# Reading K and V in runs of 32 KB that each fill two SBUF partitions

## The chip, the cores and the metric

The kernel runs on one core of one Trainium2 chip. The metric is the device time of one execution in microseconds (us); each of three runs is one time, and the median stands for the kernel. The profile is a separate execution of the same program; it counts from the first to the last instruction (its "span").

## The reference

A decode step of two branches that a gate mixes: attention over the last 2,048 keys of a cache, and a small MLP. Only the attention part reads much: K and V of 8 batches and 16 KV heads, 2,048 x 128 bf16 values each, 134.2 MB together.

```python
B, Sq, D, F = 8, 1, 576, 4608
Hq, Hkv, Sk, Dh = 32, 16, 8192, 128
W = 2048                                   # min(4096, max(256, Sk // 4))
g = sigmoid((x * gate_w).sum(-1, keepdims=True))
q = (x @ wq).reshape(B, Sq, Hq, Dh).transpose(0, 2, 1, 3)
k = repeat(k_cache[:, :, Sk - W:, :], 2, axis=1)
v = repeat(v_cache[:, :, Sk - W:, :], 2, axis=1)
p = softmax(einsum("bhqd,bhkd->bhqk", q, k) * Dh ** -0.5)
a = einsum("bhqk,bhkd->bhqd", p, v).transpose(0, 2, 1, 3).reshape(B, Sq, Hq * Dh) @ wo
b = gelu(layernorm(x) @ w1 + b1) @ w2 + b2
out = g * a + (1 - g) * b
```

## The kernel before

All SBUF data lie in one tensor, the arena. Its largest part, RAW, is cut into nine slots (`NSLOT`) of 16 KB in each of the 128 partitions, 2 MiB a slot. Everything large is streamed through these slots by loads that SyncE (SP) issues, in the order of the list `stream` (L549 to L560): five K units, then K and V units by turns, a quarter of wo (1,152 KB) behind every eighth V unit, and at the end b2 and four pieces of w2. wq and w1 are loaded first and lie where the first slots will be. SP issues a load as soon as its slot is free (`slot_free`), so several loads wait in the DMA engines' queues at any time.

One unit is one load of 2 MiB: four batches (`a`) of one KV head, 2,048 keys of 128 bf16 values each. There are 32 K units and 32 V units. `src_of` (L575) describes the source: for one batch and head the 2,048 keys are contiguous in HBM (512 KB), and it cuts them into 32 blocks `x` of 64 keys (16 KB), block outermost, batch next. The destination is a whole slot, 128 rows of 16 KB. Element order pairs the two: partition 4x + a holds block x of batch a. Both sides of one piece are 16 KB: one contiguous run in HBM, one row of the slot. A load's semaphore is complete when it has risen by 16.

A K unit (`k_unit`, L624) is transposed on VectorE in 32 x 32 blocks, half a slot at a time (L642, two instructions), and multiplied on TensorE with a block-diagonal q into PSUM (L656 to L659; the held matmuls carry the helper's line, L173). Since a row of 32 partitions holds several batches, the four heads and batches that don't belong together are pushed to a large negative score before the first K unit of a group of four: a matmul of `maskL` and `maskR` (L651). `maskR` is built once on GpSimd (L364) by an affine select over 512 columns whose pattern says to which batch a column belongs: 128 times the batches 0 to 3, one column each. Softmax follows per group of four K units (L584 to L622). A V unit (`v_unit`, L671) is used untransposed: 16 matmuls (L682) of the transposed probabilities with the slot. K and V lie in the same partition order, so the probabilities and V's rows agree.

The order on each engine comes from a planner (`_Plan.schedule`), which uses costs and due times; the loads keep the order of `stream` by `after=last_dma`.

Of the kernel before, what the change touches and what calls it, by code (L numbers as in the profile page):

```python
# [9 lines left out]
ALU = mybir.AluOpType  # L10
# [28 lines left out]
class _Plan:  # L39
# [10 lines left out]
    def add(self, eng, fn, deps=(), name=None, cost=0.1, after=(), prio=0):  # L50
        op = _Op(eng, fn, deps, name, cost, after=after, prio=prio)
        op.idx = len(self.all)
        self.all.append(op)
        return op
# [122 lines left out]
        tile_size=tile_size, tile_position=tile_position, ldweights=False))  # L177


def build_kernel(nc, A_x, A_k_cache, A_v_cache, A_wq, A_wo, B_x, B_w1, B_b1, B_w2, B_b2, gate_w, out):  # L180
    B, Sq, D = A_x.shape
    _, Hkv, Sk, Dh = A_k_cache.shape
    Hq = A_wq.shape[1] // Dh
    F = B_w1.shape[1]
    W = min(4096, max(256, Sk // 4))
    assert Sq == 1 and Dh == 128 and B == 8 and W == 2048 and Hq == 2 * Hkv and Hkv == 16
    assert D == 576 and F == 4608
    S0 = Sk - W
# [4 lines left out]
    SE = 4 * W  # L193
# [11 lines left out]
    with ExitStack() as es:  # L205
# [64 lines left out]
        AST = _pst(arena)  # L270
        arena_f = arena.bitcast(F32)

        def aoffs(name):
            return R[name][0] // 2
# [12 lines left out]
        ones_bf = view("ones_bf")  # L287
# [37 lines left out]
        def slot(s):  # L325
            return RAW[:, s * SE:(s + 1) * SE]

        wq_m = RAW[:, 0:4 * 4096].rearrange("p (t c) -> p t c", t=4)
        wq_r = RAW[:, 4 * 4096:4 * 4096 + 2048]
        W1O = 3 * SE  # L330
# [3 lines left out]
        def col(i, parts=128):  # L334
# [26 lines left out]
        o_xz0 = add("pool", lambda e: e.memset(view("xz", 8), 0.0), name="xz0", cost=0.2)  # L361
        o_yz0 = add("pool", lambda e: e.memset(view("yz", 8), 0.0), name="yz0", cost=0.2)
        o_z = add("pool", lambda e: e.memset(zeros_bf, 0.0), name="zeros", cost=0.15)
        o_mR = add("pool", lambda e: e.affine_select(out=maskR, in_=ones_bf, pattern=[[0, 128], [1, 4]], compare_op=ALU.is_equal,  # L364
                                                     fill=0.0, base=0, channel_multiplier=-1), deps=[o_ones], name="maskR", cost=0.8, prio=-1)
        o_mL = add("pool", lambda e: e.affine_select(out=maskL, in_=zeros_bf, pattern=[[0, 16], [1, 4], [0, 2]], compare_op=ALU.is_equal,
                                                     fill=-BIG, base=0, channel_multiplier=-1), deps=[o_z], name="maskL", cost=0.4, prio=-1)
# [206 lines left out]

        def src_of(cache, g, q):  # L575
            hkv, b0 = 2 * g + q // 2, 4 * (q % 2)
            return cache[b0:b0 + 4, hkv, S0:Sk, :].rearrange("a (x r) d -> x a (r d)", x=32)

        def take_slot():
            n = n_slot[0]  # L580
# [43 lines left out]
        def k_unit(i):  # L624
            g, q = divmod(i, 4)
            s = take_slot()
            d = dma("sp", lambda e: e.dma_start(slot(s), src_of(A_k_cache, g, q)), "s%d" % s, 4 * W * Dh * 2, deps=slot_free[s], name="dk%d" % i, after=last_dma[-1:])
            last_dma.append(d)
            ub = q
            qrs = []  # L630
            for a in range(4):
                def fn(e, a=a):
                    dst = bass.AP(arena, offset=32 * a * AST + aoffs("qbd") + ub * 512 + 32 * a + 8 * q, ap=[[AST, 32], [128, 4], [1, 8]])
                    src = bass.AP(arena, offset=32 * a * AST + aoffs("q4") + 32 * g + 8 * q, ap=[[AST, 32], [256, 4], [1, 8]])
                    return e.tensor_copy(dst, src)  # L635
                qrs.append(add("pool", fn, deps=[o_q4, o_qz] + [qk_unit.get(i - 4)], name="qr%d_%d" % (i, a), cost=0.2))
            trs = []
            for h in range(2):
                n = 2 * i + h
                kb = n % 2  # L640
                deps = [d] + ([qk_half[n - 2]] if n >= 2 else [o_y, o_ssq])
                tr = add("dve", (lambda h=h, kb=kb: lambda e: e.transpose(bass.AP(arena_f, offset=foffs("KT") + kb * 2048, ap=[[AST // 2, 128], [1, 2048]]),  # L642
                                                                         bass.AP(arena_f, offset=foffs("RAW") + s * (SE // 2) + 32 * h, ap=[[AST // 2, 128], [64, 64], [1, 32]])))(),
                         deps=deps, name="tr%d_%d" % (i, h), cost=2.3, after=tr_hist[-1:])
                tr_hist.append(tr)
                trs.append(tr)

                def qk_fn(e, h=h, kb=kb):
                    mm = None
                    if q == 0 and h == 0:  # L650
                        e.matmul(ps[:, 0, :], maskL, maskR, start=True, stop=False)  # L651
                        for rc in range(1, 4):
                            held_matmul(nc, e, ps[:, rc, :], maskL, maskR, start=True, stop=False)
                    for ee in range(2):
                        for rc in range(4):
                            rhs = bass.AP(arena, offset=aoffs("KT") + kb * 4096 + rc * 1024 + ee, ap=[[AST, 128], [2, 512]])  # L656
                            args = (ps[:, rc, :], qbd[:, ub, 2 * h + ee, :], rhs)
                            last = q == 3 and h == 1 and ee == 1
                            mm = e.matmul(*args, start=False, stop=last) if rc == 0 else held_matmul(nc, e, *args, stop=last)  # L659
                    return mm  # L660
                deps = [tr] + qrs
                if q == 0 and h == 0:
                    deps += exp_done[g - 1] if g else [o_q4, o_mL, o_mR]
                qk = add("pe", qk_fn, deps=deps, name="qk%d_%d" % (i, h), cost=1.95 + (0.9 if q == 0 and h == 0 else 0), after=qk_half[-1:])
                qk_half.append(qk)
            qk_unit[i] = qk
            slot_free[s] = trs
            if q == 3:
                softmax(g)

        def v_unit(i):  # L671
            g, q = divmod(i, 4)
            s = take_slot()
            item = 2 * g + q // 2
            d = dma("sp", lambda e: e.dma_start(slot(s), src_of(A_v_cache, g, q)), "s%d" % s, 4 * W * Dh * 2, deps=slot_free[s], name="dv%d" % i, after=last_dma[-1:])  # L675
            last_dma.append(d)

            def pv_fn(e):
                mm = None
                for t in range(16):  # L680
                    c = 32 * (t % 4)
                    mm = e.matmul(ps[c:c + 32, BK_OS[i % 2], :], PT[:, g % 2, 512 * q + 32 * t:512 * q + 32 * t + 32], slot(s)[:, 512 * t:512 * t + 512],  # L682
                                  start=(t < 4), stop=(t >= 12), skip_group_check=True, tile_position=(0, c))
                return mm
            deps = [d] + pt_done[g] + ([u_ev[i - 2]] if i >= 2 else [o_qT, o_u])
            prev = add("pe", pv_fn, deps=deps, name="pv%d" % i, cost=1.5, after=pv_hist[-1:])
            pv_hist.append(prev)
            slot_free[s] = [prev]
            if q == 3:
                pv_last[g] = prev  # L690
            u_ev[i] = add("act", lambda e: e.activation(out=EV[:, i % 2, :], in_=ps[:, BK_OS[i % 2], :], func=ACTF.Copy),  # L691
                          deps=[prev] + ([u_sum[i - 2]] if i >= 2 else []), name="uev%d" % i, cost=0.8, prio=3)

            def us_fn(e):
                mm = None
                for r in range(4):
                    mm = e.matmul(ps[:, BK_S, OC + 16 * (item % 2) + 8 * (q % 2):OC + 16 * (item % 2) + 8 * (q % 2) + 8], EV[:, i % 2, 128 * r:128 * r + 128], i32[:, 8 * r:8 * r + 8],  # L697
                                  start=(r == 0), stop=(r == 3), skip_group_check=True)
                return mm
            u_sum[i] = add("pe", us_fn, deps=[u_ev[i]] + o_i32 + b6_r[-2:], after=b6_w[-1:], name="us%d" % i, cost=1.0, prio=3)  # L700
            b6_w.append(u_sum[i])
            if q % 2 == 1:
                hl = q // 2
                prev = u_sum[i]
                osrc = ps[:, BK_S, OC + 16 * (item % 2):OC + 16 * (item % 2) + 16]
                if item < Hkv - 1:
                    ev = add("act", lambda e: e.activation(out=o32[:, item % 2, :], in_=osrc, func=ACTF.Copy), deps=[prev] + ([oT_done[item - 2]] if item >= 2 else []), name="oev%d" % item, cost=0.25, prio=3)  # L707
                    o_item_ev[item] = ev
                    b6_r.append(ev)
                    eng, src_, deps = "pool", o32[:, item % 2, :], [ev, rg_done[g]]  # L710
                else:
                    eng, src_, deps = "dve", osrc, [prev, rg_done[g]]

                def om_fn(e):
                    return e.tensor_tensor(out=oT[:, item, :, :].rearrange("p h b -> p b h"), in0=src_.rearrange("p (b h) -> p b h", h=2),  # L715
                                           in1=rg[:, g % 2, 16 * hl:16 * hl + 16].rearrange("p (b h) -> p b h", h=2), op=ALU.mult)
                oT_done[item] = add(eng, om_fn, deps=deps, name="oT%d" % item, cost=0.25, prio=9)
# [120 lines left out]
```

## Time and profile before

| | |
|---|---|
| median of 3 runs | 369.54 us (369.46 to 369.54) |
| profiled execution: span | 367.9 us; what lies around the span is not in the profile, and the page states no other time of this execution |
| bytes read from HBM | 154.31 MB, of them 134.2 MB K and V in 64 loads |
| PE busy | 263.5 us (72%) |
| VectorE busy | 210.4 us (57%) |
| ScalarE, GpSimd busy | 47.8 us (13%), 37.5 us (10%) |
| mean granted TensorE clock | 0.852 |

How to read it: the page's part 2 cuts the span in 40 slices of 9.2 us; its DMA row gives the busy share of the core's 16 DMA engines in tenths. Part 3 gives for each DMA queue the number of packets, their megabytes and the time that they took as a share of 16 engines over the span; q1 is the queue of SP's loads. Part 4 follows the chain of work that ended last. Beside the page, the trace keeps a list of all DMA packets (start, duration, bytes, queue) and the times at which a load's semaphore rose. Times in that list are given here from the span's start.

### The profile page before, as it was taken

The numbers are of one execution on the slowest core, as the hardware profiler recorded it, in microseconds if no ns is written. First come the engines' busy times: TensorE is split into PE (matmuls) and PEld (weight loads), VectorE is DVE, ScalarE is ACT, GpSimd is POOL, SyncE is SP. The second block draws the span as 40 slices with busy tenths as digits, with TensorE's granted clock in tenths as the row PEclk, the third lists the DMA queues.
The fourth block names the chain that finished last, engine by engine and source line by source line (L and its number), as shares of the span: only waits on it lengthen the run. The fifth ranks groups of instructions, "written<-read, shape, count | busy, mean of one in ns | idle before, by whom it ended". The sixth has DMA issues, their size and how long they took to land.

```text
span 367.9 us, 4129 instructions
## 1 busy us (share of the span) xinstructions
PE 263.5 (72%) x1837; PEld 87.0 (24%) x1429; DVE 210.4 (57%) x253; ACT 47.8 (13%) x117; POOL 37.5 (10%) x163
## 2 busy tenths in 40 slices
PE   0349984797698589773986399774976398773984
PEld 0339200122132022110321032110321032113542
DVE  0704599699686665459654674469544775364000
ACT  1010000210300220003000310003100300003200
POOL 7020011012011002000101002010110000000000
PEclk9999999699599869887897869886996879886659
DMA  8999999999999999999999999999999999999994
GB/s 345 428 412 424 435 430 433 428 428 428 433 429 431 422 433 426 428 435 427 433 431 433 408 434 432 429 426 433 433 436 428 414 434 424 431 433 440 402 429 193
DMA packets 14923, 154.59 MB, mean 420 GB/s; under 512 B 1292, under 2 KB 5428, under 8 KB 6072
## 3 DMA queue, kind: packets, MB, share of 16 engines
q1 hardware_dynamic: 14848, 154.29, 98.9%
q8 instruction: 13, 0.21, 0.2%
q10 hardware_dynamic: 56, 0.03, 0.0%
q14 instruction: 6, 0.05, 0.0%
HBM read 154.31 MB, written 0.01 MB: 419 GB/s over the span
## 4 chain that ended last, share of the span: by engine, by line
DMA 61%; PE 20%; DVE 16%; SPq 1%; issue 1%; ACT 0%; DVEq 0%; ACTq 0%
DMA arena<-in_A_k_cache_dram 50%; DMA arena<-in_B_w_dram 11%; DVE arena L642 10%; PE ps L173 9%; PE ps L659 3%; DVE arena L587 3%; PE ps L498 2%; PE ps L682 2%; PE ps L697 2%; DVE arena L606 1%; DVE arena L590 1%; PE ps L500 1%; SPq L675 1%; DVE arena L596 0%; SPq L746 0%
## 5 line engine op out<-in xcount | busy, mean ns | idle before, releaser
L642 DVE STREAM_TRANSPOSE arena<-arena 128x2048 f32<-128x2048 f32 x64 | 145.5, 2299 | 71.1 <-DMA arena<-in_A_k_cache_dram 60.1
L173 PE MATMUL ps<-arena 128*128 128x512 bf16 x408 | 141.3, 462 | 0.0
L659 PE MATMUL ps<-arena 128*128 128x512 bf16 x128 | 58.8, 459 | 21.4 <-DVE arena L642 21.3
L691 ACT ACTIVATE arena<-ps 128x512 f32<-128x512 f32 x32 | 19.1, 598 | 196.8 <-PE ps L682 196.8
L659 PEld LDWEIGHTS ps<-arena 128*128 128x128 bf16 x128 | 15.0, 117 | 124.6 <-issue 71.3
L635 POOL COPY arena<-arena 32x32 bf16<-32x32 bf16 x128 | 26.0, 203 | 159.8 <-PE ps L173 145.2
L697 PE MATMUL ps<-arena 128*128 128x8 f32 x256 | 35.3, 269 | 8.7 <-ACT arena L691 7.7
L697 PEld LDWEIGHTS ps<-arena 128*128 128x128 f32 x256 | 34.0, 208 | 21.8 <-ACT arena L691 15.2
L682 PE MATMUL ps<-arena 128*32 128x512 bf16 x512 | 36.4, 410 | 2.9 <-DMA arena<-in_A_v_cache_dram 2.9
L651 PE MATMUL ps<-arena 128*128 128x512 bf16 x8 | 4.7, 585 | 40.8 <-DVE arena L606 40.8
L587 DVE TENSOR_REDUCE arena<-ps 128x1 f32<-128x2048 f32 x8 | 18.3, 2282 | 21.6 <-PE ps L173 21.6
L601 ACT ACTIVATE arena<-ps,arena 128x512 bf16<-128x512 f32 x32 | 21.6, 686 | 40.9 <-DVE arena L596 40.9
L606 DVE STREAM_TRANSPOSE arena<-arena 128x512 bf16<-128x512 bf16 x32 | 19.9, 674 | 0.9 <-ACT arena L601 0.9
L682 PEld LDWEIGHTS ps<-arena 128*32 128x32 bf16 x512 | 11.3, 100 | 37.4 <-issue 27.1
L715 POOL TENSOR_TENSOR arena<-arena 128x16 bf16<-128x16 f32 x15 | 4.0, 266 | 141.7 <-ACT arena L707 141.7
L498 PE MATMUL ps<-arena 128*128 128x8 bf16 x144 | 10.9, 201 | 4.7 <-DMA arena<-in_B_w_dram 4.7
L541 PE MATMUL ps<-arena 128*8 128x288 bf16 (+1 forms) x140 | 11.9, 316 | 2.9 <-DMA arena<-in_B_w_dram 2.8
L498 PEld LDWEIGHTS ps<-arena 128*128 128x128 bf16 x144 | 10.8, 157 | 5.2 <-DMA arena<-in_B_w_dram 5.2
L651 PEld LDWEIGHTS ps<-arena 128*128 128x128 bf16 x8 | 0.9, 107 | 45.1 <-DVE arena L606 45.1
L613 DVE RECIPROCAL arena<-ps 128x32 f32<-128x32 f32 x8 | 2.9, 358 | 13.9 <-PE ps L611 13.9
L420 PE MATMUL ps<-arena 8*128 8x8 bf16 x8 | 0.5, 167 | 13.4 <-DVE arena L393 9.7
L715 DVE TENSOR_TENSOR arena<-ps,arena 128x16 bf16<-128x16 f32 x1 | 0.2, 229 | 16.7 <-PE ps L697 16.7
(83 smaller groups left out, 97.1 us busy)
## 6 DMA issues: line engine op xcount, KB each, us to landing
arena<-in_A_k_cache_dram SPq DMA_DIRECT2D x32, 2048.0 KB, 33.3
arena<-in_A_v_cache_dram SPq DMA_DIRECT2D x32, 2048.0 KB, 34.1
arena<-in_B_w_dram SPq DMA_DIRECT2D x1, 4608.0 KB, 24.3
arena<-in_A_wo_dram SPq DMA_DIRECT2D x4, 1152.0 KB, 36.6
arena<-in_A_wq_dram SPq DMA_DIRECT2D x1, 4096.0 KB, 13.0
arena<-in_B_w_dram SPq DMA_DIRECT2D x3, 1296.0 KB, 14.8
arena<-in_B_w_dram SPq DMA_DIRECT2D x2, 576.0 KB, 20.6
arena<-in_A_wq_dram SPq DMA_DIRECT2D x1, 512.0 KB, 3.6
```

Source lines behind the costliest of these rows:

```text
L173: return e.add_instruction(mybir.InstMatmult(name=nc.get_next_instruction_name(), engine=mybir.EngineType.PE, ins=[e.lower_ap(rhs), e.lowe ...
L498: ins = e.matmul(out_, lhsT, yT[:, kt, :], start=(kt == 0), stop=False)
L541: ins = e.matmul(ps[32 * j:32 * j + 8, BK_ACC, 0:JN], lhsT, rhs[:, JN * j:JN * j + JN], start=False, stop=True, skip_group_check=True, til ...
L587: mx = add("dve", lambda e: e.tensor_reduce(out=k(MX), in_=ps[:, 0:4, :].rearrange("p a n -> p (a n)"), axis=AXL.X, op=ALU.max), deps=[qk_ ...
L601: return e.activation(out=Pm[:, 512 * c:512 * c + 512], in_=ps[:, c, :], func=ACTF.Exp, bias=k(NB), scale=SCALE, accum_out=k(SUM + c))
L606: pts.append(add("dve", (lambda c=c: lambda e: e.transpose(bass.AP(arena, offset=aoffs("PT") + 2048 * (g % 2) + 128 * c, ap=[[AST, 128], [ ...
L635: return e.tensor_copy(dst, src)
L642: tr = add("dve", (lambda h=h, kb=kb: lambda e: e.transpose(bass.AP(arena_f, offset=foffs("KT") + kb * 2048, ap=[[AST // 2, 128], [1, 2048]]),
L659: mm = e.matmul(*args, start=False, stop=last) if rc == 0 else held_matmul(nc, e, *args, stop=last)
L682: mm = e.matmul(ps[c:c + 32, BK_OS[i % 2], :], PT[:, g % 2, 512 * q + 32 * t:512 * q + 32 * t + 32], slot(s)[:, 512 * t:512 * t + 512], st ...
L691: u_ev[i] = add("act", lambda e: e.activation(out=EV[:, i % 2, :], in_=ps[:, BK_OS[i % 2], :], func=ACTF.Copy), deps=[prev] + ([u_sum[i - ...
L697: mm = e.matmul(ps[:, BK_S, OC + 16 * (item % 2) + 8 * (q % 2):OC + 16 * (item % 2) + 8 * (q % 2) + 8], EV[:, i % 2, 128 * r:128 * r + 128 ...
```

## The change

The 32 K and 32 V loads read runs of 32 KB: the keys of one batch and head are cut into 16 blocks of 128 keys in place of 32 blocks of 64. The destination is still the whole slot, 128 rows of 16 KB, so a run of 32 KB fills two neighbouring rows. With element order as before, partition 8x + 2a + h holds half h of block x of batch a. The mask's pattern follows: 64 times the batches 0 to 3, two columns each. The load is written by a new function, `wide_load`, that puts the DMA instruction together itself with the two access patterns as they are (16 x 4 x 16,384 elements on the source side, 128 x 1 x 8,192 on the other); it goes to the same queue of SP. Nothing else differs: the number of loads, their bytes, their order and their slots, and all instructions of the other engines stay.

```diff
+def wide_load(nc, e, dst, src):
+    return e.add_instruction(mybir.InstDMACopy(
+        name=nc.get_next_instruction_name(), engine=mybir.EngineType.SP, queue="qSPDynamicHW", mode="Copy",
+        ins=e.lower_ap_dma(src), outs=e.lower_ap_dma(dst)))
...
+        def slot3(s):
+            return bass.AP(arena, offset=aoffs("RAW") + s * SE, ap=[[AST, 128], [1, 1], [1, SE]])
...
-        o_mR = add("pool", lambda e: e.affine_select(out=maskR, in_=ones_bf, pattern=[[0, 128], [1, 4]], compare_op=ALU.is_equal,
+        o_mR = add("pool", lambda e: e.affine_select(out=maskR, in_=ones_bf, pattern=[[0, 64], [1, 4], [0, 2]], compare_op=ALU.is_equal,
...
-            return cache[b0:b0 + 4, hkv, S0:Sk, :].rearrange("a (x r) d -> x a (r d)", x=32)
+            return cache[b0:b0 + 4, hkv, S0:Sk, :].rearrange("a (x r) d -> x a (r d)", x=16)
...
-            d = dma("sp", lambda e: e.dma_start(slot(s), src_of(A_k_cache, g, q)), "s%d" % s, 4 * W * Dh * 2, deps=slot_free[s], name="dk%d" % i, after=last_dma[-1:])
+            d = dma("sp", lambda e: wide_load(nc, e, slot3(s), src_of(A_k_cache, g, q)), "s%d" % s, 4 * W * Dh * 2, deps=slot_free[s], name="dk%d" % i, after=last_dma[-1:])
...
-            d = dma("sp", lambda e: e.dma_start(slot(s), src_of(A_v_cache, g, q)), "s%d" % s, 4 * W * Dh * 2, deps=slot_free[s], name="dv%d" % i, after=last_dma[-1:])
+            d = dma("sp", lambda e: wide_load(nc, e, slot3(s), src_of(A_v_cache, g, q)), "s%d" % s, 4 * W * Dh * 2, deps=slot_free[s], name="dv%d" % i, after=last_dma[-1:])
```

## The prediction

> **What bounds the kernel now.** I read the page's DMA rows first, because 154 MB in 368 us is the first thing to explain, then the chain, the waits, a window inside the K and V part, and last the trace's list of packets.
>
> ```profile
> span 367.9 us, 4129 instructions
> ...
> DMA  8999999999999999999999999999999999999994
> GB/s 345 428 412 424 435 430 433 428 428 428 433 429 431 422 433 426 428 435 427 433 431 433 408 434 432 429 426 433 433 436 428 414 434 424 431 433 440 402 429 193
> ...
> q1 hardware_dynamic: 14848, 154.29, 98.9%
> ...
> arena<-in_A_k_cache_dram SPq DMA_DIRECT2D x32, 2048.0 KB, 33.3
> arena<-in_A_v_cache_dram SPq DMA_DIRECT2D x32, 2048.0 KB, 34.1
> ```
>
> Every slice but the first and last has the DMA engines at nine tenths or more, at 402 to 440 GB/s, and SP's queue alone fills 98.9% of sixteen engines. A load lands 33 us after its issue, while one takes 4.9 us to move: six or seven loads always lie queued. So SP's issue time and the slots are not what is late.
>
> ```profile
> DMA 61%; PE 20%; DVE 16%; SPq 1%; issue 1%; ACT 0%; DVEq 0%; ACTq 0%
> ...
> DVE arena L642 <- DMA arena<-in_A_k_cache_dram: 60.1, 15, 10.5
> ...
> L642 DVE STREAM_TRANSPOSE arena<-arena 128x2048 f32<-128x2048 f32 x64 | 145.5, 2299 | 71.1 <-DMA arena<-in_A_k_cache_dram 60.1
> ```
>
> These are the chain's shares, one line of the waits (us in total, times, longest), and a group (busy and mean ns | idle before). The chain is mostly DMA, and the engine that takes K up waits 60.1 of its 71.1 idle us for K's loads; TensorE (72% busy) and VectorE (57%) have room. The kernel is bound by the rate of the stream. A stretch with K and V alone, 84 to 119 us:
>
> ```profile
> DMA packets 1041, 15.07 MB, mean 431 GB/s; under 512 B 121, under 2 KB 121, under 8 KB 121
> ...
> q1 hardware_dynamic: 1040, 15.06, 100.5%
> ```
>
> 1,041 packets less 121 of a few bytes (semaphores) are 920, one of them code on another queue: 919 x 16,384 B = 15.06 MB. Sixteen engines x 35 us x 100.5% = 562.8 us, over 919 packets 612 ns each. The packet list says the same more sharply: 8,151 of the 8,192 K and V packets took 611 ns, and on one engine they start 607.4 ns apart (the next begins a little before the last ends). 128 packets of 32,768 B (wq) took 1,213 ns in the median and start 1,209.6 ns apart.
>
> **What the change costs, step by step.**
>
> (1) *Fewer reads.* 32 KB as two packets: 2 x 607.4 = 1,214.8 ns; as one: 1,209.6 ns. So 16 KB more cost 602.2 ns (27.2 B/ns for one engine, 435 GB/s for sixteen) and a packet has about 5.2 ns of its own. An engine moves 128 KiB of each load (the semaphore rises in 16 steps), now 8 packets, then 4: 4 x 5.2 = 21 ns a load, x 64 = 1.3 us less. The trace has no packet that fills two rows. Upper bound of the gain: the full 1.3 us (the 5.2 ns belong to the read); lower: nothing (they belong to each row filled, and there are still 8). I take 1.2, being nearest to the wq row, whose packets are also counted one by one. The wq row also has a bad side: its 4 MB took 9.97 us by the first engine's landings, 421 GB/s, against 431 for K; by that rate 64 loads would take 8.0 us more (134.2 MB at 421 and at 431 GB/s). That is the stretch in which code and the small inputs are loaded too, and its later packets run at 1,213 ns, so I leave it to the range.
>
> (2) *Which engine writes where.* Before, 32 outer blocks over 16 engines give each engine two blocks of four rows. Now there are 16 outer blocks for 16 engines: one block each, that is eight neighbouring partitions. This is the step that no row prices directly. Before, the engines visibly never meet: 8,151 equal durations, although the engines run out of step with one another. The step can cost nothing (each engine still reaches the rows at its own rate), or, at worst, engines meet in pairs at the same rows' entrance all the time; two at an entrance that takes one engine's 27.2 B/ns need 2 x 602.2 ns for 16 KB each.
>
> [...] I take 1.9 for the slowest pair over the run, 1.6 to 2.0 as its range.
>
> Added: 64 x (1.9 - 1) x 8 x 602.2 ns = 277 us (185 at 1.6, 308 at 2.0). Nothing hides it: the DMA chain is the path. What is late next is K at L642, whose 60.1 us of waiting would grow by about that.
>
> [...]
>
> (3) *The mask.* L364 takes 1.55 us at 5.3 us with a pattern of two terms; with three terms I bound it by nothing and by its double. It ends before 10 us, and its first users run at 12.2 us (L526) and about 38.65 us (L651): 2 us of cover. Uncovered it would cost 1.55.
>
> (4) *SP's issue.* 64 issues of some 0.54 us, between nothing and double: 35 us at most over the run, against 4.86 us between landings and 33 us of queue. Zero.
>
> (5) *VectorE, TensorE, ScalarE, GpSimd:* same instructions, shapes and order; zero.
>
> Sum against the profiled execution: 367.9 - 1.2 + 277 = 643.7 us of span. The median of runs is 1.6 us above the span, which I keep: 645.
>
> **The rivals.**
>
> [...]
>
> *B. Fewer reads, no meeting: faster.* Place: each engine's packet train in K and V. Price: 21 ns x 64. It decides if the entrances take more than one engine's rate, or the share of an engine is still divided as before. 369.5 - 1.2 = 368.3 us (down to 368.2). For: wq's 32 KB packets at 1,213 ns; the stream is at 431 of 435 GB/s, so packets' own time is all that is left to take. Against: it needs step 2 to be free.
>
> *C. The change does nothing to the time.* Two rows per read pay the 5.2 ns twice, or each run is split in two again: 369.5 us. The packet counts would tell the two apart. For: 8 rows are still filled.
>
> **How the numbers follow.** Steady meeting 0.37, A 0.26, B 0.28, C 0.09. Meeting gets the most because the code leaves no other division of 16 blocks over 16 engines; B keeps over a quarter because no trace here shows that neighbouring rows share anything. The likeliest is steady meeting, 645 us; its own range is 550 to 677. A measurement of this kernel can tell 0.2% (0.7 us) from no change: B at 368.3 is 0.34% faster. Faster 0.28, same 0.09, slower 0.63. The whole range must reach B, so 367.9 to 677.
>
> **What would show it.** In the changed kernel's profile, 16 KB packets give way to 4,096 of 32 KB (14,848 packets in q1 less 4,096). Steady meeting: K and V slices at 220 to 280 GB/s with the DMA row still at 9, packets of about twice 1,213 ns, L642's wait near 340 us, PE busy share down to some 40%. [...] B: slices at 432 to 434, packets at 1,213 ns, landings 4.84 us apart. C: landings 4.86 apart. Slices at 420 with no doubled packets would mean that long reads themselves are slower (step 1), and I would be wrong in a way not listed.

## The result, and the profile after

The changed kernel took 664.49 us in the median of 6 runs (657.04 to 668.69), the kernel before 369.50 us (369.40 to 369.54, 6 runs) on the same chip: a ratio of 1.790, 95% interval 1.784 to 1.797. The ratio leaves out the two longest of the six runs (668.28, which is the profiled one, and 668.69 us) as slow ones. The profiled execution took 668.28 us, with a span of 666.5 us.

The changed kernel's page, its rows of slices, its queue and its chain (first lines of the last: shares by engine; lines of the code stand nine further down than before, so L642 is now L651):

```profile
span 666.5 us, 4129 instructions
...
PE 322.4 (48%) x1837; PEld 99.5 (15%) x1429; DVE 209.7 (31%) x253; ACT 47.9 (7%) x117; POOL 38.6 (6%) x163
...
DMA  9999999999999999999999999999999999999996
GB/s 391 331 216 217 210 221 212 221 220 220 218 231 220 239 215 224 226 228 227 223 220 228 218 236 231 236 231 222 232 230 227 211 228 230 219 224 224 227 240 250
...
q1 hardware_dynamic: 10752, 154.29, 99.2%
...
another core or an unknown queue 36%; DMA 29%; PE 18%; DVE 14%; issue 1%; SPq 1%; ACTq 0%; POOL 0%; DVEq 0%
```

The DMA row stands at nine as before, the bytes are the same 154.29 MB, and there are 14,848 - 10,752 = 4,096 packets fewer. But from the third slice on each moves 210 to 250 GB/s where it moved some 430. The DMA engines are as busy as before (q1 fills 99.2% of sixteen engines, 98.9% before) and get half as far. What the chain calls "another core or an unknown queue" (36%) this page leaves unexplained; the waits in the next view name K's loads.

The waits on a tile, and the group that takes K up (us in total, times, longest; busy, mean ns | idle before):

```profile
DVE arena L651 <- DMA arena<-in_A_k_cache_dram: 350.7, 31, 17.9
...
L651 DVE STREAM_TRANSPOSE arena<-arena 128x2048 f32<-128x2048 f32 x64 | 144.9, 2294 | 350.8 <-DMA arena<-in_A_k_cache_dram 350.7
```

The transposes cost what they did (2,294 ns against 2,299). VectorE waits before them 350.7 us for K in place of 60.1, which is 290.6 of the 298.6 us that the span has grown.

One stretch of 80 to 120 us (us, then busy time and count of PE, PEld, DVE, ACT and POOL, PE's granted clock, DMA share, GB/s), first of the kernel before, then of the changed one:

```profile
80.00:120.00 40.00, 33.52 (x211) 9.22 (x144) 30.85 (x30) 6.22 (x16) 4.97 (x24) 0.86 1.01 430
```

```profile
80.00:120.00 40.00, 20.05 (x90) 3.64 (x55) 18.36 (x25) 3.98 (x10) 1.62 (x8) 0.67 1.01 219
```

In the same 40 us TensorE runs 90 matmuls and not 211, and the clock it is granted falls from 0.86 to 0.67. The DMA engines are full in both rows. In the packet list K's and V's 4,096 packets of 32,768 B have a median of 2,346 ns (mean 2,349; 5% to 95%: 2,167 to 2,542), while wq's packets of the same size, loaded before, took 1,213.

### The profile page after: what moved, and what is told of

It reads as the page before. It is cut to its first block, busy times and chain, and to the rows that moved or that the text cites. A ratio compares the mean times of both kernels' runs of the same rounds, so it can differ in the third digit from the quotient of the medians.

```text
span 666.5 us, 4129 instructions
## 1 busy us (share of the span) xinstructions
PE 322.4 (48%) x1837; PEld 99.5 (15%) x1429; DVE 209.7 (31%) x253; ACT 47.9 (7%) x117; POOL 38.6 (6%) x163
## 3 DMA queue, kind: packets, MB, share of 16 engines
q1 hardware_dynamic: 10752, 154.29, 99.2%
## 4 chain that ended last, share of the span: by engine, by line
another core or an unknown queue 36%; DMA 29%; PE 18%; DVE 14%; issue 1%; SPq 1%; ACTq 0%; POOL 0%; DVEq 0%
DMA arena<-in_A_k_cache_dram 25%; PE ps L173 10%; DVE arena L651 9%; PE ps L668 4%; DMA arena<-in_B_w_dram 3%; DVE arena L596 2%; PE ps L691 2%; DMA arena<-in_B_b_dram 1%; PE ps L706 1%; DVE arena L615 1%; PE ps L473 1%; DVE arena L605 1%; SPq L755 1%; DVE arena L599 0%
## 5 line engine op out<-in xcount | busy, mean ns | idle before, releaser
L651 DVE STREAM_TRANSPOSE arena<-arena 128x2048 f32<-128x2048 f32 x64 | 144.9, 2294 | 350.8 <-DMA arena<-in_A_k_cache_dram 350.7
L173 PE MATMUL ps<-arena 128*128 128x512 bf16 x408 | 170.1, 542 | 0.0
L668 PE MATMUL ps<-arena 128*128 128x512 bf16 x128 | 71.3, 557 | 151.5 <-DVE arena L651 151.5
L691 PE MATMUL ps<-arena 128*32 128x512 bf16 x512 | 44.9, 484 | 92.6 <-DMA arena<-in_A_v_cache_dram 92.6
L668 PEld LDWEIGHTS ps<-arena 128*128 128x128 bf16 x128 | 17.2, 134 | 285.5 <-DVE arena L651 193.7
L706 PE MATMUL ps<-arena 128*128 128x8 f32 x256 | 45.0, 308 | 8.7 <-ACT arena L700 7.7
L706 PEld LDWEIGHTS ps<-arena 128*128 128x128 f32 x256 | 44.1, 262 | 26.4 <-ACT arena L700 14.6
L660 PE MATMUL ps<-arena 128*128 128x512 bf16 x8 | 4.8, 605 | 63.3 <-DVE arena L651 53.2
L507 PE MATMUL ps<-arena 128*128 128x8 bf16 x144 | 11.0, 201 | 7.4 <-DMA arena<-in_B_w_dram 7.4
L507 PEld LDWEIGHTS ps<-arena 128*128 128x128 bf16 x144 | 10.8, 157 | 7.9 <-DMA arena<-in_B_w_dram 7.9
L660 PEld LDWEIGHTS ps<-arena 128*128 128x128 bf16 x8 | 0.8, 104 | 68.3 <-DVE arena L651 55.8
L550 PEld LDWEIGHTS ps<-arena 128*8 128x8 bf16 (+1 forms) x140 | 6.1, 97 | 14.6 <-issue 7.3
L509 PE MATMUL ps<-arena 128*128 128x8 bf16 x36 | 7.2, 200 | 0.0
```

The costliest lines, as they stand in the source:

```text
L173: return e.add_instruction(mybir.InstMatmult(name=nc.get_next_instruction_name(), engine=mybir.EngineType.PE, ins=[e.lower_ap(rhs), e.lowe ...
L507: ins = e.matmul(out_, lhsT, yT[:, kt, :], start=(kt == 0), stop=False)
L550: ins = e.matmul(ps[32 * j:32 * j + 8, BK_ACC, 0:JN], lhsT, rhs[:, JN * j:JN * j + JN], start=False, stop=True, skip_group_check=True, til ...
```

## The experiments

Two things changed at once: the reads became longer and filled two rows each, and the load was cut into 16 outermost blocks and not 32. The theory on record, called M below, blames the second: with 16 blocks there is one for each of the 16 engines, eight neighbouring rows, and engines hinder each other in pairs. Which engine writes which rows is in no trace, since the packet list names no engine; one block an engine is worked out from the code (16 blocks, and a load's semaphore rises in 16 steps). The pairs are the author's assumption, and so is what M says of a lead d of one partner over the other: a factor of 2 - d/T, from 2 in step down to 1 half a share apart. T = 4 x 602.2 ns = 2.41 us is the time in which an engine alone moves 64 KiB, half its share of a load. The runs with leads test both. Times in packet lists are counted from the span's start.

**Division alone.** The kernel before with its own reads of 16 KB and the plain load, but cut into 16 blocks: a load takes half the keys of all eight batches of a head. The attention it computes is not the reference's, since the rest isn't adapted.

```diff
-            hkv, b0 = 2 * g + q // 2, 4 * (q % 2)
-            return cache[b0:b0 + 4, hkv, S0:Sk, :].rearrange("a (x r) d -> x a (r d)", x=32)
+            hkv, k0 = 2 * g + q // 2, S0 + W // 2 * (q % 2)
+            return cache[:, hkv, k0:k0 + W // 2, :].rearrange("a (x r) d -> x a (r d)", x=16)
```

> The kernel before with its plain loads and runs of 16 KB, one per row, but cut as 16 outer blocks x 8 batches (half the keys of each) in place of 32 blocks x 4 batches; the mask is as before, so the attention mixes batches and the result is not the reference's. Theory M (16 outer blocks hand each engine eight neighbouring rows, and engines meet in pairs): as slow as the change, 16 KB packets of about 1,160 ns in place of 611, 620 to 690 us. Theory R (a read of 32 KB that fills two rows is itself slow): 369.5 us, packets of 611 ns. Theory H (sixteen engines reading HBM 32 KB apart are slow; here they read 16 KB apart as before): 369.5 us.

Measured: 673.14 us (670.60 to 679.15), 1.824 times the kernel before (1.816 to 1.832). Its row of the same 40 us:

```profile
80.00:120.00 40.00, 18.53 (x88) 3.39 (x54) 19.41 (x25) 3.92 (x10) 1.63 (x8) 0.71 1.01 218
```

It moves 218 GB/s with packets of 16 KB that took 1,202 ns in the median where the kernel before has 611. K's and V's reads are as short as before and fill one row each, so neither long reads nor reads over two rows are needed for the loss.

**Long reads alone.** The changed kernel with `wide_load`, its 32 KB reads and two rows per read, but 32 blocks: two batches, 4,096 keys of each. It reads other keys than the window, so again its attention is not the reference's.

```diff
-            return cache[b0:b0 + 4, hkv, S0:Sk, :].rearrange("a (x r) d -> x a (r d)", x=16)
+            return cache[b0:b0 + 2, hkv, Sk - 2 * W:Sk, :].rearrange("a (x r) d -> x a (r d)", x=32)
```

> The changed kernel's load function, runs of 32 KB and two rows per read, but 32 outer blocks x 2 batches (4,096 keys of each, half of them outside the window) in place of 16 blocks x 4 batches; bytes per load and the 32 KB distance of the blocks are those of the change, the attention is not the reference's. Theory M: no meeting, so full speed: packets of 1,213 ns, 368.3 us if the 5.2 ns of a packet belong to the read, 369.5 if to each row. Theory R: as slow as the change, 640 to 680 us. Theory H: as slow as the change, 640 to 680 us.

Measured: 368.55 us (368.51 to 368.57) beside 369.61, a ratio of 0.9972 (0.9958 to 0.9986). Its page:

```profile
GB/s 346 429 434 420 434 444 415 444 418 445 418 441 436 407 429 448 418 447 419 438 432 425 406 458 415 450 416 440 432 429 441 417 420 445 418 440 440 388 431 184
...
q1 hardware_dynamic: 10752, 154.29, 98.5%
```

The packet count is that of the changed kernel and the rate that of the kernel before. Packets took 1,213 ns in the median. Long reads are harmless here and save 1.06 us.

**The same bytes, 32 blocks.** The run above reads other keys. This one reads the same 134.2 MB as the changed kernel, in the same reads of 32 KB, but a load takes 256 keys of 32 neighbouring pairs of batch and head.

```diff
-            hkv, b0 = 2 * g + q // 2, 4 * (q % 2)
-            return cache[b0:b0 + 4, hkv, S0:Sk, :].rearrange("a (x r) d -> x a (r d)", x=16)
+            j, y = divmod(4 * g + q, 8)
+            pairs = cache.rearrange("b h s d -> (b h) s d")
+            return pairs[32 * j:32 * j + 32, S0 + 256 * y:S0 + 256 * (y + 1), :].rearrange("x (o r) d -> x o (r d)", o=2)
```

> The changed kernel with the same 134.2 MB of the window in the same 32 KB reads, each filling two rows, but each load takes 256 keys of 32 neighbouring (batch, head) pairs (4 batches... of a load are replaced by 2 batches x 16 heads), so that 32 blocks stand outermost and not 16. The rest of the kernel is not adapted to that order, so the attention it computes is not the reference's; number and bytes of loads, and all other instructions are those of the changed kernel. Theory 'the number of outermost blocks decides': packets of 1,213 ns, 368.3 to 368.8 us, ratio 0.996 to 0.998 of before. Rival 'the pitch of the source decides' (blocks 2 MB apart in HBM instead of 32 KB): packets above 1,300 ns, more than 380 us.

Measured: 368.46 us (368.31 to 368.74, 8 runs) beside 369.51, a ratio of 0.9973 (0.9962 to 0.9984), packets of 1,213 ns. So it isn't the keys, nor the pitch, the distance of the blocks in HBM, which was 32 KB in the run before and is 2 MB here.

**The source or the rows?** Sixteen blocks again, of eight rows each, but with the source of the last run: the blocks are the 16 heads of a batch, 2 MB apart, and not 32 KB apart.

```diff
-            hkv, b0 = 2 * g + q // 2, 4 * (q % 2)
-            return cache[b0:b0 + 4, hkv, S0:Sk, :].rearrange("a (x r) d -> x a (r d)", x=16)
+            return cache[g, :, S0 + 512 * q:S0 + 512 * (q + 1), :].rearrange("x (o r) d -> x o (r d)", o=4)
```

> The changed kernel with the same 134.2 MB in the same 32 KB reads and 16 outermost blocks of eight rows, but the blocks of a load are the 16 heads of one batch (512 keys each), which lie 2 MB apart in HBM, as in the run with 32 pairs, and not 32 KB apart. The rest of the kernel is not adapted to that order, so the attention it computes is not the reference's. Theory 'the rows that an engine writes decide': the source does not matter, packets of 2,200 to 2,500 ns from the first load on, 640 to 680 us. Rival 'the reads decide' (sixteen engines that read in step 32 KB apart collide in HBM): packets of 1,213 ns, 368 to 370 us.

Measured: 659.53 us (659.03 to 660.03), a ratio of 1.785 (1.780 to 1.790); 2,315 ns in the median. The last two runs in the view of 80 to 120 us, first 32 blocks 2 MB apart, then 16:

```profile
80.00:120.00 40.00, 31.93 (x200) 8.71 (x132) 29.62 (x30) 6.21 (x16) 4.85 (x23) 0.87 1.00 432
```

```profile
80.00:120.00 40.00, 20.98 (x95) 4.18 (x58) 17.52 (x24) 3.98 (x10) 1.62 (x8) 0.68 1.01 222
```

Same read size, same pitch in HBM, same rows filled in all: 432 against 222 GB/s. Both pitches, 32 KB and 2 MB, are now measured with both numbers of blocks: slow with 16 blocks (1.790 and 1.785), not with 32 (0.997 twice). What differs is the number of outermost blocks, and the pitch is refuted as the cause. With the number of blocks it may also change which reads an engine makes; that the loss is not on that side is argued from the copies inside HBM below. The 16 engines are full with either number (shares of 1.01 with 16 blocks and 1.00 with 32). Full is not enough.

**Leads.** If engines hinder each other because they go through their rows in step, then shifting some of them should part them. Small copies from HBM to HBM, whose result nobody uses, are put on SP's queue between w1's last piece and the first K load, on some of the engines only (the packets below show the number: beside a copy of twelve blocks K starts on four engines, beside one of four blocks on the other twelve; that a copy of k blocks uses the first k engines is assumed). A copy of 64 KB per engine took 2,418 ns in the median, about the T = 2.41 us of half a share. The edit, here the lines of one copy on twelve engines:

```diff
         last_dma = [d_w1r]
...
+        jk0 = nc.dram_tensor("jk0", (16, 33280), BF, kind="Internal").ap()
+        d_jk0 = dma("sp", lambda e: e.dma_start(jk0[0:12, 0:32768], A_wq[0:9 * 12, :].rearrange("(k r) c -> k (r c)", r=9)[:, 0:32768]), "jk0", 131072, name="d_jk0", after=last_dma[-1:])
+        last_dma.append(d_jk0)
...
```

First a copy on twelve engines and then a second on four (64 KB each), so that four engines start K without delay, eight half a share later and four a whole share later:

> The changed kernel with two extra copies inside HBM on SP's queue ahead of the first K load: 64 KB on each of twelve engines, then 64 KB on each of four. If they go to the lowest-numbered engines, as theory M takes it, engines 0 to 3 and 8 to 11 start K by T = 2.4 us behind their partners 4 to 7 and 12 to 15. Theory M with a lead that stays: partners are half a share apart, the factor is 1.0 to 1.2 for the slowest pair, K packets near 1,213 ns at the start: 372 to 435 us. Theory N (the division of rows costs the same however the engines stand to each other): 664 us plus 2 to 5, 666 to 670.

Measured: 477.9, 501.9, 517.1 and 523.0 us, between the two theories' ranges. Rows of the profiled run, which is the fastest (477.9):

```profile
28.00:32.00 4.00, 4.00 (x70) 4.00 (x69) 0.00 (x0) 0.00 (x0) 0.41 (x2) 1.00 1.04 430
34.00:38.00 4.00, 4.00 (x70) 4.00 (x69) 0.00 (x0) 0.00 (x0) 0.00 (x0) 1.00 0.92 270
60.00:64.00 4.00, 0.39 (x3) 0.10 (x1) 2.72 (x2) 0.00 (x0) 0.81 (x4) 1.00 1.06 352
80.00:84.00 4.00, 4.00 (x23) 0.81 (x15) 1.90 (x3) 0.00 (x0) 0.10 (x1) 0.78 1.01 336
90.00:94.00 4.00, 4.00 (x31) 0.76 (x20) 1.87 (x1) 0.60 (x1) 0.46 (x3) 1.00 0.89 311
```

At first all is clean: 430 GB/s with the same 16 blocks, and K's packets that begin up to 30.4 us took 1,213 to 1,286 ns, first on four engines, from 28 us on up to twelve. From 31.0 us on all sixteen read K, and on fourteen of them the packets that begin from 30.7 to 32.3 us still took only 1,224 to 1,320 ns. That shows that the loss is one of timing between engines, not of the layout by itself.

Two engines fell out first: their packets that begin at 30.72 and 30.78 us took 1,818 and 2,011 ns. One of the two had been last with w1 and began K only at 29.57 us, at least 1.0 us behind the other seven with the same lead; by M its partner was then no longer half a share away. A packet of code, on another queue, came at 31.9 us; the K packets that begin from 32.8 us on took 1,540 to 2,412 ns, on all engines, and later grew shorter, by the median of 3 us from 1,824 ns at 34 us to 1,446 at 73. Whether the late engine or the code packet spread the loss to all is not shown. Of later code packets, the one at 94.4 us is followed by longer K packets (1,473 ns in the median of the 4 us before, 1,606 behind), the one at 41.6 us is not (1,787 and 1,813). So with a lead the loss is away at first; it comes, and wears off slowly (1,824 ns to 1,446), as in the forecast's A, engines that meet but move apart, though only where a lead was given.

One copy on eight engines, to see who the partners are:

> The changed kernel with one extra copy inside HBM ahead of the first K load: 64 KB on each of eight engines, by theory M engines 0 to 7, so both partners of a pair (e and e + 4) are late by the same. Theory M with partners four apart: no gain, 660 to 675 us. Theory M8 (partners are eight apart): all pairs are half a share apart, 372 to 435 us. Theory N: 664 plus 2, about 667 us.

Measured: 679.07 us (677.45 to 680.28), ratio 1.837 (1.834 to 1.840). Call the groups of four engines, in the order in which the copies are taken to fill them, A, B, C and D. Here C and D run together, half a share ahead of A and B, and the loss is full from the second K packet of C and D on (2,469 to 2,506 ns). In the run before, B and C ran together without loss, and A and D were on the same half of their share. So if engines meet in pairs, C's partner is D, with 2,445 ns (the median at 60 to 100 us) where the two are in step, and not B, with 1,213 ns for B and C in step in the run before. That leaves B for A, by elimination alone: engines e and e + 4.

Half the lead, and twice the lead:

> As e3, with copies of half the size: engines 0 to 3 and 8 to 11 start K by T/2 = 1.2 us behind their partners. Theory M with a lead that stays as it is: factor 1.5, K packets about 1,815 ns all along, 369.5 + 64 x 0.5 x 4.82 + 2 = 526 us (480 to 590). Theory M with a lead that grows by itself when partners are part apart: packets that start near 1,815 ns and get shorter, 440 to 530 us. Theory N: 664 to 668 us.

> As e3 with each of the two copies made twice (to places of their own): the same engines start K by 2T = 4.8 us behind, a whole share, so partners are one load apart and again at the same half. Theory M (what counts is the place within the share): in step again, 660 to 690 us. If any lead helps, as in e3: 480 to 530 us. Theory N: 670 us, which this run alone can't tell from M.

Measured: 628.82 to 665.00 us (median 647.27, four runs) for half, 538.14 to 660.53 (median 596.74, four runs) for double. Neither is what was expected. With half a lead K's packets took 2,296 ns in the median from 30 to 40 us, where M's 2 - d/T, with d = T/2, gives 1.5 x 1,213 = 1,820. With the double lead the first packets took 1,213 ns and those from 32 to 40 us 2,314 in the median. The double lead scatters too widely to say whether loads in a row are tied to each other.

**Who is slowed?** The copy on A's four engines alone:

> As e3 with the small copy alone: only engines 0 to 3 start K by T behind, so the pairs with 4 to 7 are half a share apart and the pairs of 8 to 15 are in step. Theory M with pairs that don't touch each other: K packets of two kinds, half near 1,213 to 1,600 ns and half near 2,400; each load waits for the slow half, so no gain: 645 to 680 us. Theory G (what is shared is shared by all sixteen engines): one kind of packet in between, 560 to 620 us.

Measured: 673.24 and 551.49 us. The packets (those of the run of 673.24) decide. In the list K's packets come in waves, here with the us at which they begin, how many, and the ns they took:

```
25.70 to 26.08   11   1,695 to 2,060   B, C, D: first packets (one engine is still at w1)
27.39 to 28.13   12   2,473 to 2,529   B, C, D: second (at 28.04 the late engine's first)
28.14 to 28.58    4   2,012 to 2,067   A: first
29.86 to 30.64   16   2,240 to 2,329   all
32.11 to 32.89   16   2,411 to 2,431   all
```

Expected were two kinds of packets side by side: C and D slow, B at 1,213 as long as its partner A is away. There is nearly one kind, and none at 1,213. B was slowed with the rest. If a packet goes at full speed up to some moment c and at half speed from then on, it takes 2 x 1,213 ns less the time from its start to c; for ten of the eleven first packets that gives one and the same c, 26.42 to 26.45 us, some 0.7 us after the first start. So the change from 1 to 2 came to all that read K at once.

Two more rows of this list say where the loss lies. The late engine's w1 packets of 4,608 B, which write other rows in another shape, took 178 ns up to 25.98 us and 325 to 353 from 26.4 us on; in the run below, where nothing meets at that time, such packets on its late engine stay at 178. And A's four copies, which go from HBM to HBM while the others read K at half speed, took 2,418 ns each, as they do without a meeting. So what is slow lies on the way into SBUF and not in reading HBM: w1's load into SBUF is slowed, the copies inside HBM are not. (In the run with the double lead, eight such copies beside slow K packets took 2,494 to 3,102 ns, somewhat longer, but not twice as long.)

The counterpart, made to test just that: the copy on A, B and C, so that D is alone.

> The changed kernel with one copy of 64 KB on each of engines 0 to 11 ahead of the first K load (HBM to HBM, 12 packets, as in the earlier lead runs the first of the two copies; the output is the reference's). Engines 12 to 15 start K at about 26 us with nobody beside them, the other twelve 2.4 us later. Theory 'a meeting slows all sixteen': 12 to 15 read at 1,213 ns until about 28.2 us; from then on engines 0 to 7 meet in step, and all sixteen, 12 to 15 included, show equal packets of 2,200 to 2,500 ns at the same time; 640 to 680 us. Rival 'closed pairs', the prediction's picture (an engine is slowed only by its own partner): 8 to 15 are half a share apart from their partners and stay at 1,213 to 1,850 ns while 0 to 7 are at 2,300 to 2,430, so two kinds of packets stand side by side; the time is still that of the slowest, 640 to 680 us. The packets decide, not the time.

Measured: 615.36 and 663.39 us. Packets of the run of 615.36:

```
25.78 to 27.23    8   1,213 to 1,276   D: first and second packets
28.05 to 28.44   15   1,595 to 2,000   all but one engine, whose copy runs until 29.62
29.62 to 30.44   16   2,145 to 2,579   all (15 of them 2,549 or more)
31.75 to 32.99   16   2,246 to 2,289   all
```

D runs at 1,213 ns alone, also beside the others' copies. A and B then start in step; C follows D by half a share, so by M neither of those two is with its partner. All slow down alike, and 14 of the 15 packets of the second wave give one moment again: 28.85 to 28.89 us. Closed pairs are refuted: in these two runs engines without a partner beside them are slowed as much as those that meet. It isn't so at every moment: in the run with the full lead two engines were slowed for some 2 us before the other fourteen.

## Why the prediction came out right, and where it was wrong

The time was 664.5 us where 645 was forecast, by the likeliest case. By its steps:

- **Fewer reads, -1.2 us.** Right. The runs with 32 blocks show it alone: 1.06 and 1.05 us less. A packet's own time belongs to the read and not to each row filled; otherwise these runs would have shown nothing, as rival C had it. The bad side, 421 GB/s for wq, was not the long reads: they ran at 432.
- **Which engine writes where.** Right as far as it can be seen, and this is the step that makes the result: 16 blocks of 16 KB reads are slow (1.824), 32 blocks of 32 KB reads are not (0.997), at one pitch and read size (1.785 against 0.997). The runs show the number of blocks; which rows an engine writes, and whether rows have an entrance that engines share, none of them shows.
- **The factor, 1.9.** Somewhat low. No run shows the term itself, a factor of the slowest pair. What the runs show in its place is the mean packet of all engines, 2,349 ns, against 1,209.6 from start to start unhindered: 1.94. By the term of the sum, 0.94 x 308.3 = 290 us and not 277.
- **A term that was left out.** wo is loaded between K and V by loads that did not change, yet the 4,104 packets of 1,152 B (4,096 of wo, eight of b2) took 85.9 ns in the mean and not 51.1: 34.8 x 4,104 / 16 = 8.9 us. The sum had only K and V in it. wo doesn't lose by itself: its packets took 51 ns in the median while no packet of K or V was in flight, and 93 while two were. With the two corrections it gives 367.9 - 1.2 + 290 + 8.9 = 665.6, against a span of 666.5.
- **Who hinders whom: closed pairs, with M's 2 - d/T.** Wrong. Half a lead cost nearly as much as none (2,296 ns, not 1,820), and an engine without a partner beside it is slowed as much as those that have one. The slowest pair didn't have to be picked out: in these two runs there is none. That the number came out near is luck to this extent: the engines start almost in step (in the changed kernel fourteen begin their first K packet between 25.61 and 25.99 us), and there both pictures, pairs and all sixteen, give about 2.
- **Steady or moving apart.** In the changed kernel it stays: 2,441 ns in the median at 60 to 100 us, 2,396 at 100 to 200, 2,348 at 500 to 600. What A stood for, a loss that wears off, exists: from the full lead the packets go from 1,824 ns down to 1,446 within some 40 us. Here, where nothing had set the engines apart, there is only the 4% just given. Its 0.26 was not absurd: with copies ahead of K the same loads took 478 to 680 us.
- **Mask, SP's issue, the other engines: nothing.** Right: transposes at 2,294 ns against 2,299, VectorE busy 209.7 us against 210.4.
- **The signs.** Packets (10,752), slices (mostly 210 to 240, the lower ones below the 220 that I gave), DMA row at nine, L651's wait (350.7, forecast near 340) came as written. PE's busy share did not: 48% and not 40%. The share was worked out with unchanged matmul times, but the granted clock fell from 0.852 to 0.69, and the held matmuls took longer:

```profile
L173 PE MATMUL ps<-arena 128*128 128x512 bf16 x408 | 141.3, 462 | 0.0
...
L173 PE MATMUL ps<-arena 128*128 128x512 bf16 x408 | 170.1, 542 | 0.0
```

The first line is the kernel before, the second the changed one: 542 ns each and not 462, with no idle time put down to a wait before them. Here the slower stream went with a lower clock too, but it costs nothing: PE idles half the time.

What stays open is what the engines share on the way into SBUF that lets a meeting of some slow them all, why it took some 2 us to spread in the run with the full lead, and whether a code packet on one engine can set it off. No version beyond the kernel before was found that computes the reference's result in less time: the two layouts at 368.5 us take K and V in an order for which the rest of the kernel would have to be written anew, for 0.3%.

## What to carry to other kernels

A load can keep all 16 DMA engines full and still run at half its rate (a share of 1.01 at 219 GB/s and at 430). What decided it in this kernel was the number of outermost blocks on the source side, 16 or 32 (1.785 against 0.997), and, as the run with the full lead shows, when the engines start on them (430 GB/s at first with the same 16 blocks). Before changing the shape of a load, see into how many outermost blocks it falls, 32 of four rows or 16 of eight, and compare the time of one packet with that of the same size elsewhere in the trace. A packet saved was worth 4 to 5 ns of one engine's time here (1.05 us x 16 / 4,096 = 4.1), too little to risk the number of blocks for.

## What was not expected of the hardware

A meeting of some engines can slow all sixteen, bystanders too, in two runs from one instant on (26.42 to 26.45 us, 28.85 to 28.89), 0.4 to 0.8 us after the engines that meet have started; in a third, two engines were slow for some 2 us before the rest. It reaches loads of other shapes: wo's packets of 1,152 B took a median of 91 ns in place of 51, w1's last packets of 4,608 B 325 to 353 in place of 178. Copies from HBM to HBM at the same time are not slowed (2,418 ns) or much less (up to 3,102). And the same 16 blocks run without the loss (430 GB/s) at first with the full lead, about 5 us of the one run that was profiled with it.
